# A linear-attention and ReGLU kernel on one core: half-row first loads, a first group made on TensorE, sketches in 16 tiles, one store per group, and a fixed issue order

## The chip, the cores and the metric

The kernel runs on one core of a Trainium2 chip. The metric is device time in microseconds (us) of that core, start to end of one execution of the program. Shapes are fixed. Engines are named as in the profile: PE is TensorE, DVE VectorE, ACT ScalarE, POOL GpSimd, and SP the sequencer that issues most DMAs.

## What is computed

```python
batch, n_heads, seq, head_dim = (4, 4, 1088, 32);  r = 8
def phi(x):
    a = np.einsum('rd,bhsd->bhsr', S1, x)
    b = np.einsum('rd,bhsd->bhsr', S2, x)
    return np.einsum('bhsi,bhsj->bhsij', a, b).reshape(*x.shape[:-1], r * r)
q_p, k_p = (phi(q), phi(k))
kv = np.einsum('bhsf,bhsd->bhfd', k_p, v)
z = np.sum(k_p, axis=2)
num = np.einsum('bhsf,bhfd->bhsd', q_p, kv)
den = np.einsum('bhsf,bhf->bhs', q_p, z)[..., None] + 1e-06
attn = num / den
x = attn.transpose(0, 2, 1, 3).reshape(4352, 128)
out = (np.maximum(x @ w_gate, 0.0) * (x @ w_val)) @ w_out     # d_ff = 1536
```

Two sketches of eight columns each make 64 features per head (phi). Sums over all tokens of a batch give kv and z, so no row of attn of a batch can be made before all of its k and v has gone through. The result, 4352 tokens of 128, goes through a gated feed-forward network (FFN) of width 1536. Inputs and output are float32; features and FFN are fp16 inside.

## The kernel before

**Tokens.** The 1088 tokens of a batch are 34 chunks of 32 rows, each row of SBUF holding one head's row of 34 x 32 numbers. Thirty-two chunks form 8 columns of four (x = 0 to 7), two are left over. The FFN takes tokens in ten groups, written (batch, first x, number of x): (0,0,2), (0,2,2), (0,4,4), then (b,0,4) and (b,4,4) for b = 1 to 3, and a group of 256 that collects the left-over chunks of all batches. The first group is small, so that the FFN may begin early.

**k side, class K, once a batch.** DVE transposes k in 32 x 32 blocks (L389, L393, L397). PE makes both sketches with the block-diagonal weights wS (L405, L416: 64-row by 32-column tiles, eight of which cover the array), DVE transposes back (kt2, L425). PE sums z (L434), DVE copies it (L442), PE and DVE make of z a third sketch matrix wc (L445, L450), by which q gives the denominator. The feature products kphi (L456) are made on DVE and POOL, ACT casts v to fp16 (L462, L466), PE makes kv (L473), DVE masks and scales it (L480).

**q side, class Q, once a group.** PE makes the two sketches (L586) and the third (L595) from the transposed q; DVE transposes back (L603, L611); the product of second and third sketch (L617, bw), its sum (L624), the reciprocal (L629) and the division of the first sketch by it (L633) follow, then the feature product (L640). Early groups do these on DVE, the others on POOL. The features are transposed by PE and ACT (L656, L661) for batch 0, by a DMA (L648) for the rest; PE multiplies by kv (L669, L676), and ACT writes xT (L684).

**FFN, class F.** 102 units of 512 result columns: PE makes the gate (g, L730) and the value (v, L741), ACT takes relu of g (L735), DVE multiplies it with v (h, L750). In 13 units ACT copies v (L746) and POOL multiplies (L754). Four matmuls of w_out (L761) add up in one PSUM bank per group; ACT scales that into SBUF (oe, L769), and SP stores it: four DMAs of 32 rows a group (L776), eight for the left-over group (L784).

**What sets the order.** Each step is an operation of a planner (class Plan) with a cost, a due time and PSUM banks to lease from seven; a list scheduler fixes at build time the order in which each engine's instructions are issued. Matmuls of zeros (L263) go to the eighth bank: 34 at the start, six after the S matmuls, and as many as fit into planned gaps of PE ahead of the first FFN matmul, 100 in all.

**Loads.** ACT and SP each issue one load of S1 and S2 (L203, L204). SP then loads k of batch 0 whole (L205) and q of batch 0 in three parts (L220, L221, L223); ACT's queue loads v (L189, L195). POOL's loads the weights: w_gate and w_val in three blocks of four column tiles each (L236, L237), w_out in one. A `gate` copy on POOL (L799) holds back the loads of the later batches (L805, L808), which SP issues.

Of the kernel before, what the change touches and what calls it, by code (L numbers as in the profile page):

```python
# [17 lines left out]
EPS = 1e-6  # L18


class Lease:


    def __init__(self, n=1):
        self.n, self.banks, self.free_at, self.left = n, None, None, 0


class Op:
    def __init__(self, eng, name, busy, vis, fn, after, take, drop, due):
        self.eng, self.name, self.busy, self.vis, self.fn = eng, name, busy, vis, fn  # L30
        self.after = [a for a in after if a is not None]
        self.take, self.drop, self.due = take, drop, due
        self.succ, self.start, self.done, self.seq = [], None, None, None


class Plan:


    HOLD = 1.0
    LAT = {"PE": 0.20, "DVE": 0.035, "ACT": 0.035, "POOL": 0.06, "SP": 0.0, "DMA": 0.05}  # L40

    def __init__(self, free, banks):
        self.free = dict(free)
        self.banks = {b: 0.0 for b in banks}
        self.ops = []

    def add(self, eng, name, busy, fn, after=(), take=(), drop=(), rec=0.0, due=None):
        op = Op(eng, name, busy, busy + rec + self.LAT[eng], fn, after, take, drop, due)
        op.seq = len(self.ops)
        for l in drop:  # L50
            l.left += 1
        for a in op.after:
            a.succ.append(op)
        self.ops.append(op)
        return op

    def look(self, o):
        return 0.0

    def landed(self, name, at):  # L60
        op = self.add("DMA", name, 0.0, None)
        op.start, op.done = at, at
        return op

    def dues(self, slack):
        for op in reversed(self.ops):
            lim = [s.due - op.vis - slack(op, s) for s in op.succ if s.due is not None]
            if op.due is not None:
                lim.append(op.due)
            op.due = min(lim) if lim else 1e6  # L70

    def run(self):
        todo = [o for o in self.ops if o.start is None]
        need = {o: sum(a.start is None for a in o.after) for o in todo}
        ready = [o for o in todo if not need[o]]
        n = 0
        while ready:
            for o in ready:
                o.at = max([self.free[o.eng]] + [
                    a.start + a.busy if a.eng == o.eng == "PE" else a.done for a in o.after])  # L80
            have = sorted(self.banks.values())
            now = min(o.at for o in ready)

            held = 0
            wants = sorted((o for o in ready if any(l.banks is None for l in o.take)),
                           key=lambda o: (o.due, o.seq))
            for o in wants:
                w = sum(l.n for l in o.take if l.banks is None)
                near = o.at <= now + self.HOLD
                if held + w > len(have):  # L90
                    o.at = None
                else:
                    o.at = max(o.at, have[held + w - 1])
                if near:
                    held += w
            can = [o for o in ready if o.at is not None]
            if not can:
                raise RuntimeError("no bank for any of " + ", ".join(o.name for o in ready))
            o = min(can, key=lambda o: (o.at, o.due, o.seq))

            o = min((c for c in can if c.eng == o.eng and c.at <= o.at + self.look(o)),
                    key=lambda c: (c.due, c.seq))
            o.start = o.at
            o.done = o.start + o.vis
            self.free[o.eng] = o.start + o.busy
            for l in o.take:
                if l.banks is None:
                    got = sorted(self.banks, key=lambda b: (self.banks[b], b))[:l.n]
                    l.banks = sorted(got)
                    for b in got:  # L110
                        del self.banks[b]
            for l in o.drop:
                l.left -= 1
                l.free_at = max(l.free_at or 0.0, o.done)
                if not l.left:
                    for b in l.banks:
                        self.banks[b] = l.free_at
            ready.remove(o)
            for s in o.succ:
                need[s] -= 1  # L120
                if not need[s]:
                    ready.append(s)
            n += 1
        assert n == len(todo), [o.name for o in todo if o.start is None]
        return max(o.done for o in todo)
# [3 lines left out]
def kernel(  # L129
# [25 lines left out]
    LAG = 3  # L155
# [3 lines left out]
    f_g = ctx.enter_context(tc.tile_pool(name="f_g", bufs=6))  # L159
    f_h = ctx.enter_context(tc.tile_pool(name="f_h", bufs=10))  # L160
# [6 lines left out]


    s16 = sb([2 * R, 4, D], FP32, "s16")
    k_sb = [sb([128, NC * D], FP32, f"k_sb{b}") for b in range(B)]  # L170
    q_sb = [sb([128, NC * D], FP32, f"q_sb{b}") for b in range(B)]
    v32 = [sb([128, H, NX * D], FP32, f"v32_{b}") for b in range(B)]
# [3 lines left out]
    wv = sb([DM, NJ, 128], FP16, "wv")  # L176
    wo = sb([128, NJ, DM], FP16, "wo")
# [4 lines left out]
    xT = sb([HD, B * NX * 128 + 256], FP16, "xT")  # L182


    def flat(src, b):
        return src[b].rearrange("h (p c) d -> (h p) (c d)", c=NC)

# [12 lines left out]
    def wcols(w, lo, hi):  # L200
        return w.rearrange("m (j f) -> m j f", j=NJ)[:, lo:hi]

    nc.scalar.dma_start(out=s16[0:R], in_=S1[:, None, :].to_broadcast([R, 4, D]))  # L203
    nc.sync.dma_start(out=s16[R:2 * R], in_=S2[:, None, :].to_broadcast([R, 4, D]))  # L204
    nc.sync.dma_start(out=k_sb[0], in_=flat(k, 0))  # L205
    zero = sb([128, 128], FP16, "zero")
    nc.vector.memset(zero, 0.0)
    scr = sb([1, 1], FP16, "scr")
    nc.scalar.activation(out=scr, in_=zero[0:1, 0:1], func=ACTF.Relu)
    for a in range(4):  # L210
        load_v(nc.scalar, 0, a)
    for a in range(2):
        load_vr(nc.scalar, a, 0, 1)

    Q0 = 2 * D

    def by_x(t, lo, hi):
        return t[:, 0:4 * NX * 32].rearrange("p (a c) -> p a c", a=4)[:, :, lo * 32:hi * 32]

    nc.sync.dma_start(out=by_x(q_sb[0], 0, 2), in_=by_x(flat(q, 0), 0, 2))  # L220
    nc.sync.dma_start(out=by_x(q_sb[0], 2, NX), in_=by_x(flat(q, 0), 2, NX))  # L221
    qrest = slice(4 * NX * 32, NC * 32)
    nc.sync.dma_start(out=q_sb[0][:, qrest], in_=flat(q, 0)[:, qrest])  # L223

    id16 = sb([2 * R, 2 * R], FP32, "id16")
    make_identity(nc, id16)
    sel = sb([2 * R, 16, R], FP32, "sel")
    nc.gpsimd.tensor_copy(out=sel, in_=id16[:, None, 0:R].to_broadcast([2 * R, 16, R]))
    maskl = sb([128, 4, 4], FP32, "maskl")
    nc.gpsimd.memset(maskl, 1.0)  # L230
    nc.gpsimd.affine_select(out=maskl, in_=maskl, compare_op=ALU.is_ge, fill=0.0, base=0,
                            pattern=[[-8, 4], [-32, 4]], channel_multiplier=1)
    nc.gpsimd.affine_select(out=maskl, in_=maskl, compare_op=ALU.is_ge, fill=0.0, base=R - 1,
                            pattern=[[8, 4], [32, 4]], channel_multiplier=-1)
    for lo in range(0, NJ, 4):
        nc.gpsimd.dma_start(out=wg[:, lo:lo + 4], in_=wcols(moe_w_gate, lo, lo + 4))  # L236
        nc.gpsimd.dma_start(out=wv[:, lo:lo + 4], in_=wcols(moe_w_val, lo, lo + 4))  # L237
    nc.gpsimd.dma_start(out=wo, in_=moe_w_out.rearrange("(j f) m -> f j m", f=128))
    ident = sb([128, 128], FP16, "ident")
    make_identity(nc, ident)  # L240


    maskp = sb([128, 2], FP32, "maskp")
    maskw = sb([128, H, R], FP32, "maskw")
    maskkv = sb([128, 2, D], FP32, "maskkv")
    nc.vector.memset(maskp, 0.0)
    nc.vector.memset(maskw, 0.0)  # L247
    nc.vector.memset(maskkv, 0.0)
    for h in range(H):
        nc.vector.memset(maskp[32 * h:32 * h + 32, h % 2:h % 2 + 1], 1.0)  # L250
        nc.vector.memset(maskw[32 * h:32 * h + 32, h], DSCALE)
    for i in range(2):
        nc.vector.memset(maskkv[64 * i:64 * i + 64, i], KVSCALE)
    NBW = 3
    bw = [sb([128, GX * H, R + 1], FP32, f"bw{i}") for i in range(NBW)]
    for i in range(NBW):
        nc.vector.memset(bw[i][:, :, R], EPS * DSCALE)

    W_BANK = 7
# [31 lines left out]
    def pe16(n, cols):  # L291
        return n * max(cols / 2400.0 + 0.0025, 0.0285)
# [626 lines left out]
```

## Time and profile before

| what | value |
|---|---|
| time, median of 3 runs | 121.84 us (121.58 to 121.86) |
| span of the profiled execution | 119.8 us |
| time of a run outside that span (median less span) | 2.0 us |
| busy: PE, PEld, DVE, ACT, POOL | 105.0, 69.6, 85.9, 79.4, 60.8 us |
| first FFN matmul (L730) | 21.11 us |
| last instruction of ACT ahead of the last stores | 113.51 us |

The profile is one execution, taken by the hardware profiler. Busy time is summed per engine; PEld are the weight loads, which overlap the matmuls. The chain of waits is followed back from the last instruction to what released it, step by step, and gives each engine and line a share of the span. The timeline gives start, duration, engine, line, operation, result and operands of each instruction or run of equal ones; `[0.39 <-PE ...]` behind it says how long the engine stood idle before it and who released it. The stretches give busy time of each engine, number of instructions in brackets, the granted PE clock and the DMA share. The DMA view counts packets by size and, for each queue, packets, MB and the share of the time of all 16 DMA engines in the stretch.

### The profile page before, as it was taken

How to read it: one execution, taken by the hardware profiler on the slowest of the kernel's cores; microseconds unless marked ns; L12 is line 12 of the kernel's file. 1: busy time of each engine (PE TensorE's matmuls, PEld its weight loads, DVE VectorE, ACT ScalarE, POOL GpSimd, SP SyncE). 2: the span in 40 equal slices, each digit the busy share in tenths (PEclk: the TensorE clock that was granted, in tenths of full speed). 3: DMA queues.
4: the chain of work that ended last, by engine and by line, in shares of the span. 5: the costliest groups of instructions: out<-in, count | busy, mean ns of one | idle time of the engine just before them, and what ended most of it. 6: DMA issues, size and time to landing. Idle time of an engine off the chain costs nothing.

```text
span 119.8 us, 3483 instructions
## 1 busy us (share of the span) xinstructions
PE 105.0 (88%) x1354; PEld 69.6 (58%) x1354; DVE 85.9 (72%) x196; ACT 79.4 (66%) x152; POOL 60.8 (51%) x75
## 2 busy tenths in 40 slices
PE   6966996998997959989999899998999999999600
PEld 6954866795755626445566564665656656569300
DVE  2169558599997969988999586876858858776600
ACT  4003102899785855869958669896799799998500
POOL 7938206800967189636542997595095262332100
PEclk9999999999999999999999999999999999999985
DMA  2999999999931508230421071105204302300310
GB/s 48 273 229 218 204 312 252 275 242 307 242 90 32 108 0 50 43 88 0 87 68 25 10 86 45 45 5 112 63 0 96 88 3 44 70 23 0 88 27 16
DMA packets 17104, 12.02 MB, mean 100 GB/s; under 512 B 11456, under 2 KB 15296, under 8 KB 17088
## 3 DMA queue, kind: packets, MB, share of 16 engines
q1 hardware_dynamic: 13768, 10.07, 37.6%
q0 software_dynamic: 2416, 1.18, 7.3%
q10 hardware_dynamic: 904, 0.56, 2.2%
q8 instruction: 10, 0.16, 0.7%
q14 instruction: 6, 0.05, 0.2%
HBM read 9.05 MB, written 2.23 MB: 94 GB/s over the span
## 4 chain that ended last, share of the span: by engine, by line
PE 69%; DMA 8%; ACT 7%; DVE 7%; issue 2%; DVEq 1%; ACTq 0%
PE ps L730 19%; PE ps L741 17%; PE ps L761 17%; DMA v<-in_v_dram 7%; ACT g_sb L735 3%; PE ps L595 3%; PE ps L586 3%; PE ps L473 3%; PE ps L669 2%; DVE kab L425 2%; ACT v L462 2%; DVE qab L603 2%; PE ps L434 1%; DMA s<-in_S_dram 1%; DVE ht L750 1%
## 5 line engine op out<-in xcount | busy, mean ns | idle before, releaser
L735 ACT ACTIVATE g_sb<-ps 128x512 f16<-128x512 f32 x102 | 58.4, 610 | 15.3 <-PE ps L730 13.0
L750 DVE TENSOR_TENSOR ht<-g_sb,ps 128x512 f16<-128x512 f16 x89 | 57.4, 678 | 13.1 <-PE ps L730 5.5
L730 PE MATMUL ps<-xT,wg 128*128 128x512 f16 (+1 forms) x120 | 38.8, 348 | 2.7 <-DVE kab L425 1.5
L741 PE MATMUL ps<-xT,wv 128*128 128x512 f16 (+1 forms) x120 | 38.8, 348 | 0.7 <-DVE kab L425 0.4
L761 PEld LDWEIGHTS <-ht 128*128 128x128 f16 x408 | 28.6, 98 | 17.2 <-issue 3.1
L761 PE MATMUL ps<-wo,ht 128*128 128x128 f16 x408 | 36.8, 219 | 0.8 <-DVE ht L750 0.4
L754 POOL TENSOR_TENSOR ht<-g_sb,v_sb 128x512 f16<-128x512 f16 x13 | 15.0, 1156 | 15.1 <-ACT v_sb L746 15.0
L456 POOL TENSOR_TENSOR kp<-kab 128x512 f16<-128x512 f32 (+1 forms) x14 | 16.4, 1200 | 8.7 <-DVE kab L425 8.7
L640 POOL TENSOR_TENSOR qqp<-qan,qab 128x1024 f16<-128x1024 f32 (+2 forms) x10 | 16.4, 1643 | 5.5 <-DVE qan L633 5.0
L741 PEld LDWEIGHTS <-wv 128*128 128x128 f16 x120 | 11.3, 98 | 6.9 <-issue 3.8
L730 PEld LDWEIGHTS <-wg 128*128 128x128 f16 x120 | 11.6, 99 | 4.7 <-issue 2.3
L263 PE MATMUL ps<-zero 128*128 128x128 f16 x100 | 9.7, 272 | 1.1 <-DVE maskw L247 1.1
L633 POOL TENSOR_TENSOR qan<-qab,qrd 128x128 f32<-128x128 f32 (+1 forms) x8 | 3.1, 394 | 13.8 <-DVE qrd L629 10.9
L462 ACT CAST v<-v 128x512 f16<-128x512 f32 x8 | 4.7, 628 | 7.9 <-DMA v<-in_v_dram 7.9
L263 PEld LDWEIGHTS <-zero 128*128 128x128 f16 x100 | 8.2, 125 | 1.8 <-DVE maskw L247 1.1
L746 ACT CAST v_sb<-ps 128x512 f16<-128x512 f32 x13 | 7.7, 590 | 0.0
L603 DVE STREAM_TRANSPOSE qab<-ps 128x256 f32<-128x256 f32 (+1 forms) x10 | 4.0, 405 | 4.7 <-PE ps L595 2.7
L473 PEld LDWEIGHTS <-kp 128*128 128x128 f16 (+1 forms) x72 | 4.8, 107 | 3.4 <-issue 1.7
L473 PE MATMUL ps<-v,kp 128*128 128x64 f16 (+1 forms) x72 | 5.6, 204 | 1.3 <-ACT v L462 1.0
L661 ACT COPY qpt<-ps 128x512 f16<-128x512 f16 (+1 forms) x3 | 2.2, 727 | 6.9 <-PE ps L656 6.8
L617 POOL TENSOR_TENSOR bw<-qab,qc 128x128 f32<-128x128 f32 (+1 forms) x8 | 3.5, 440 | 6.0 <-DVE qc L611 5.0
L769 ACT ACTIVATE o_sb<-ps 128x512 f32<-128x512 f32 (+1 forms) x10 | 5.5, 550 | 1.4 <-PE ps L761 1.4
(70 smaller groups left out, 86.1 us busy)
## 6 DMA issues: line engine op xcount, KB each, us to landing
k_sb<-in_k_dram SPq DMA_DIRECT2D x4, 544.0 KB, 6.6
out_dram<-o_sb SPq DMA_DIRECT2D x28, 64.0 KB, 1.7
q_sb<-in_q_dram SPq DMA_DIRECT2D x3, 544.0 KB, 7.8
v<-in_v_dram SPq DMA_DIRECT2D x12, 128.0 KB, 7.2
v<-in_v_dram ACTq DMA_DIRECT2D x4, 128.0 KB, 5.4
wg<-in_moe_w_gate_dram POOLq DMA_DIRECT2D x3, 128.0 KB, 8.4
q_sb<-in_q_dram SPq DMA_DIRECT2D x1, 384.0 KB, 9.1
wv<-in_moe_w_val_dram POOLq DMA_DIRECT2D x3, 128.0 KB, 8.6
```

The source lines that it names most:

```text
L263: nc.tensor.matmul(PS[:, W_BANK, 0:128], zero, zero, start=True, stop=True)
L456: eng.tensor_tensor(out=self.kp[:, lo:hi].rearrange("p x g (i a c) -> p (x g i) a c", i=2, a=R), in0=src[:, 0, :, :, None].to_broadcast([1 ...
L462: nc.scalar.copy(out=v16[self.b][:, 2 * h:2 * h + 2, 0:NX * D], in_=v32[self.b][:, 2 * h:2 * h + 2])
L473: nc.tensor.matmul(m[:, 64 * p:64 * p + 64], self.kp[rows, x, p], v16[self.b][rows, 2 * p:2 * p + 2, x * D:(x + 1) * D], start=(x == 0 and ...
L640: eng.tensor_tensor(out=self.qp[:, lo:hi].rearrange("p x g (i a c) -> p (x g i) a c", i=2, a=R), in0=self.an[:, lo * H:hi * H, :, None].to ...
L730: nc.tensor.matmul(bank(self.lg)[:, y * W:(y + 1) * W], wg[:, j], x, start=True, stop=True, skip_group_check=True)
L735: nc.scalar.activation(out=self.gs, in_=bank(self.lg), func=ACTF.Relu)
L741: nc.tensor.matmul(bank(self.lv)[:, y * W:(y + 1) * W], wv[:, j], x, start=True, stop=True, skip_group_check=True)
L746: nc.scalar.copy(out=self.vs, in_=bank(self.lv))
L750: nc.vector.tensor_tensor(out=self.ht, in0=self.gs, in1=bank(self.lv), op=ALU.mult)
L754: nc.gpsimd.tensor_tensor(out=self.ht, in0=self.gs, in1=self.vs, op=ALU.mult)
L761: nc.tensor.matmul(o[:, s], self.ht[:, y * W + s * 128:y * W + (s + 1) * 128], wo[:, j], start=(j == 0 and s == 0), stop=(j == NJ - 1), sk ...
```

## The change

- **Order.** The list scheduler goes. A table START gives the rank of every operation, BANKS the PSUM banks of each lease (all eight now), WARM the places of 39 matmuls of zeros in place of 100. Dependencies are as the code states them; each engine takes its operations by rank.
- **First loads.** k and q of batch 0 are loaded in two parts of half rows (`half`, L256), the first half holding 16 chunks; v of batch 0 in eight smaller loads. In SP's order the first half of k is followed by that of q. Both loads of S go to ACT's queue.
- **First group.** Class First makes the features of group (0,0) directly in the layout that kv needs: `feat` (L645) multiplies q with sketch matrices that are widened to all 64 pairs (wab), once for the first and once for the second factor; ACT copies one, DVE multiplies (L616). The transposes of features by PE go there. The denominator is made on its own path (the first sketch with z, L673), turned into a [feature, token] tile by a widened copy, a PE transpose and a copy, and multiplied in where x is written (L637), behind kv.
- **k side of batch 0.** For two of the kphi products ACT copies the second sketch to PSUM (L533), and DVE reads it there (L539).
- **q sketches.** Once a batch, not once a group, all three sketches side by side as one matrix wq of 32 columns; 16 matmuls of 32 rows by 32 columns by 256 tokens (L761). Transposes, sums and reciprocals of a batch's both groups are made together.
- **Weights.** wg and wv are laid out [128, 3, 128, 4] and read by PE with a step of 4 elements (L884), so that each of their loads is one run per row; w_out comes in three loads.
- **Stores.** One DMA for a group of 128 x 512 (L927), two on SP and two on ACT for the left-over group (L933).
- **Buffers.** g_sb 8 in place of 6, ht 12 in place of 10; k_sb and v32 two in place of four, shared by b and b + 2. Thirteen units go to POOL as before, others of them.

The core of the diff:

```diff
-    def run(self):
-        todo = [o for o in self.ops if o.start is None]
...
+    def run(self, warm):
+        order = sorted(self.ops, key=lambda o: (START[o.seq] if START else 0, o.seq))
+        for o in order:
+            if o.seq in WARM:
+                warm(WARM[o.seq])
+            o.fn()
...
-    wg = sb([DM, NJ, 128], FP16, "wg")
+    wg = sb([DM, 3, 128, 4], FP16, "wg")
...
-    nc.sync.dma_start(out=k_sb[0], in_=flat(k, 0))
+    def half(t, src, y):
+        lo, hi = (0, CY) if y == 0 else (CY, NC * D)
+        return lambda: nc.sync.dma_start(out=t[:, lo:hi], in_=flat(src, 0)[:, lo:hi])
...
+        def feat(self, l, w):
+            for p in range(2):
+                rows = slice(64 * p, 64 * p + 64)
+                for x in range(self.n):
+                    nc.tensor.matmul(
+                        bank(l, p)[:, x * 128:(x + 1) * 128], wab[rows, w].rearrange("p g i j -> p (g i j)"),
+                        by_x(qT[0], x, x + 1)[rows], start=True, stop=True,
+                        skip_group_check=True)
...
+            rb = P.add("ACT", "f rb", lambda: nc.scalar.copy(
+                out=self.rb, in_=self.rd[:, :, None].to_broadcast([128, n * H, D])), [o3])
+            rt = P.add("PE", "f rt", lambda: self.rt(lx), [rb, fidf], take=[lx])
...
+            self.x_op = P.add("DVE", "f x", lambda: nc.vector.tensor_tensor(
+                out=xT[:, 0:n * 128], in0=bank(ln)[:, 0:n * 128], in1=self.rT, op=ALU.mult),
...
+        def sk(self, ls):
+            for h in range(H):
+                rows = slice(32 * h, 32 * h + 32)
+                o = bank(ls[h // 2], h % 2)
...
+                            nc.tensor.matmul(
+                                o[32 * a:32 * a + 32, (lo - self.x0) * 32:(hi - self.x0) * 32],
+                                wq[self.b][rows, h],
...
-                nc.tensor.matmul(bank(self.lg)[:, y * W:(y + 1) * W], wg[:, j], x,
+                nc.tensor.matmul(bank(l)[:, y * self.W:(y + 1) * self.W], w[:, j // 4, :, j % 4],
...
-                for a in range(4):
-                    nc.sync.dma_start(
-                        out=out[b * S:(b + 1) * S].rearrange("(p c) m -> p (c m)", c=NC)[
-                            :, (a * NX + x0) * DM:(a * NX + x0 + n) * DM],
-                        in_=self.os[32 * a:32 * a + 32, 0:n * DM])
+                dst = rows.rearrange("p (a x) m -> a p x m", a=4)[:, :, x0:x0 + n]
+            nc.sync.dma_start(out=dst.rearrange("a p x m -> a p (x m)"),
+                              in_=self.os[:, 0:n * DM])
...
+                eng.dma_start(
+                    out=out[b * S:(b + 1) * S].rearrange("(p c) m -> p c m", c=NC)[
+                        :, 4 * NX:NC].rearrange("p e m -> e p m"),
+                    in_=self.os[p0:p0 + 64, y * DM:(y + 1) * DM])
```

More of the change, by code (lines that the diff above doesn't have):

```diff
@@ L31, in __init__ @@
         self.after = [a for a in after if a is not None]
-        self.take, self.drop, self.due = take, drop, due
-        self.succ, self.start, self.done, self.seq = [], None, None, None
+        self.take, self.drop = take, drop
 class Plan:
[L39 to L53, printed above, removed]
+    def __init__(self):
+        self.ops, self.leases = [], []
@@ L54, in add @@
+    def add(self, eng, name, fn, after=(), take=(), drop=()):
+        op = Op(eng, name, fn, after, take, drop, len(self.ops))
         self.ops.append(op)
         return op
[L57 to L70, printed above, removed]
@@ L72, in run @@
-    def run(self):
-        todo = [o for o in self.ops if o.start is None]
[L74 to L125, printed above, removed]
@@ L235 @@
[L235 to L246, printed above, removed]
@@ new lines, with fill4 @@
+    f3 = P.add("DVE", "sel", fill3, [fid, f0])
+    def fill4():
+        nc.vector.tensor_reduce(out=mz, in_=maskl, axis=AX.X, op=ALU.add)
+    f4 = P.add("DVE", "mz", fill4, [fml])
+    l_s, l_x = Lease(P), Lease(P)
+    st_op = P.add("PE", "st", lambda: nc.tensor.matmul(
+        bank(l_s)[:, 0:2 * R], s16.rearrange("f p d -> f (p d)"), id16, start=True, stop=True),
+        [ls1, ls2, fid, f0], take=[l_s])
+    ws_op = P.add("DVE", "ws", lambda: nc.vector.tensor_tensor(
+        out=wS, in0=bank(l_s)[:, 0:2 * R].rearrange("p (w i) -> p w i", w=2)[
+            :, :, None, :].to_broadcast([128, 2, 2, R]),
+        in1=maskp[:, None, :, None].to_broadcast([128, 2, 2, R]), op=ALU.mult), [st_op, f1])
@@ new lines, with mk_wq @@
+    s1r_op = P.add("POOL", "s1r", mk_s1r, [stc, f1])
+    sx_op = P.add("PE", "sx", lambda: nc.tensor.matmul(
+        bank(l_x)[:, 0:D], sel.rearrange("f a i -> f (a i)"), s16[:, 0], start=True, stop=True),
+        [ls1, ls2, f3], take=[l_x])
+    l_op = P.add("ACT", "L", lambda: nc.scalar.copy(
+        out=L, in_=bank(l_x)[:, None, 0:D].to_broadcast([128, H, D])), [sx_op], drop=[l_x])
+    def mk_wq(b):
+        nc.gpsimd.memset(wq[b][:, :, 24:32], 0.0)
+        nc.gpsimd.tensor_copy(
+            out=wq[b][:, :, 0:16],
+            in_=s_t.rearrange("p w i -> p (w i)")[:, None, :].to_broadcast([128, H, 2 * R]))
@@ new lines, in __init__ @@
+            for (lo, hi, rest), t1 in zip(parts, t1s):
+                la = Lease(P, 2)
+                s = P.add("PE", f"ksk {b} {lo}",
+                          lambda la=la, lo=lo, hi=hi, rest=rest: self.sk(la, lo, hi, rest),
+                          t1 + [ws_op, f2], take=[la])
+                self.sks.append(s)
+                self.t2s.append(P.add(
+                    "DVE", f"kt2 {b} {lo}",
+                    lambda la=la, lo=lo, hi=hi + rest: self.t2(la, lo, hi), [s] + pu, drop=[la]))
@@ new lines, in vcr, with kv @@
+        def vcr(self):
+            nc.scalar.copy(out=v16[self.b][0:64, :, NX * D:KX * D], in_=vr32[:, self.b])
+        def kv(self, lm, lo, hi):
+            m = bank(lm)
+            for x in range(lo, hi):
+                for p in range(2):
+                    nc.tensor.matmul(
+                        m[:, 64 * p:64 * p + 64], self.kp[:, x, p],
+                        v16[self.b][:, 2 * p:2 * p + 2, x * D:(x + 1) * D],
+                        start=(x == 0 and p == 0), stop=(x == NX), skip_group_check=True)
@@ new lines, in t2, with at @@
+        def t2(self, la):
+            nc.vector.transpose(
+                self.ab.rearrange("p w x h f -> p h x w f"),
+                pair(la)[:, :, 0:self.n * 32].rearrange("p h (x w f) -> p h x w f", w=2, f=16))
+        def at(self, l):
+            for x in range(self.n):
+                nc.tensor.matmul(
+                    bank(l)[:, x * 128:(x + 1) * 128], s1r.rearrange("p r h i -> p (r h i)"),
+                    by_x(qT[0], x, x + 1), start=True, stop=True, skip_group_check=True)
@@ new lines, in csk, with mul @@
+        def csk(self, lc):
+            for x in range(self.n):
+                nc.tensor.matmul(
+                    bank(lc)[:, x * 32:(x + 1) * 32], self.aT[:, x * 128:(x + 1) * 128],
+                    self.kk.zs.rearrange("p h r -> p (h r)"), start=True, stop=True,
+                    skip_group_check=True)
+        def mul(self, lc):
+            nc.vector.tensor_tensor(
+                out=self.bw[:, :, 0:R],
+                in0=self.ab[:, 1].rearrange("p x g (i r) -> p (x g i) r", r=R),
+                in1=bank(lc)[:, 0:self.n * 32].rearrange("p (x r) -> p x r", r=R), op=ALU.mult)
@@ L666, in num, with tre @@
+        def tre(self, lt, lo, m):
+            o = bank(lt).bitcast(FP16)
+            nc.scalar.copy(out=self.pt[:, lo:lo + m].rearrange("f x g t -> f (x g t)"),
+                           in_=o[:, 0:m * 256])
+        def num(self, ln, lo, m):
+            o = bank(ln)
             for p in range(2):
@@ L857, with warm @@
-    P.ops.sort(key=lambda o: o.seq)
-    order, seen = [], set()
-    def visit(o):
-        if o in seen:
-            return
-        seen.add(o)
-        for a in o.after:
-            visit(a)
-        order.append(o)
-    import sys
-    sys.setrecursionlimit(100000)
-    for o in P.ops:
-        visit(o)
-    P.ops = order
-    P.dues(slack)
-    end = P.run()
+    def warm(n):
+        for _ in range(n):
+            nc.tensor.matmul(PS[:, 7, 0:128], zero, zero, start=True, stop=True,
+                             skip_group_check=True)
@@ L876 @@
     if __name__ != "kernel":
         kernel.plan = P
-        kernel.end = end
-    todo = sorted((o for o in P.ops if o.fn), key=lambda o: (o.start, o.seq))
-    f0 = min(o.start for o in P.ops if o.name.startswith("g "))
-    at = None
-    for o in todo:
-        if o.eng == "PE":
-            if at is not None and o.start < f0 + 0.1 and o.start - at > 0.3:
-                warm(int((o.start - at - 0.1) / 0.065))
-            at = o.start + o.busy
-        o.fn()
+        if not START:
+            return
@@ L892 @@
+    P.run(warm)
 _INS = ['q', 'k', 'v', 'S1', 'S2', 'moe_w_gate', 'moe_w_val', 'moe_w_out']
```

983 lines of the change are left out of this document (500 added, 483 removed), and 70 rows, old and new, of tables (BANKS, START).

## The prediction

> **What bounds the kernel now.** I read the chain of waits first, then the timeline up to the first FFN matmul, the busy time by stretches, and the DMA view of the first loads and of the end.
>
> ```profile
> PE 105.0 (88%) x1354; PEld 69.6 (58%) x1354; DVE 85.9 (72%) x196; ACT 79.4 (66%) x152; POOL 60.8 (51%) x75
> PE 69%; DMA 8%; ACT 7%; DVE 7%; issue 2%; DVEq 1%; ACTq 0%
> ```
>
> PE carries 69% of the chain, so the end is set by PE's stream; the shares are averages over three stages, which I cost apart.
>
> ```profile
> 6.24 1.29 DVE L389 STREAM_TRANSPOSE kT<-k_sb 128x512 f32<-128x512 f32 x2
> ...
> 16.66 0.32 DVE L603 STREAM_TRANSPOSE qab<-ps 128x128 f32<-128x128 f32 x1 [1.16 <-PE ps L595]
> ...
> 20.69 0.37 ACT L684 CAST xT<-ps 128x256 f16<-128x256 f32 x1 [0.39 <-PE ps L669]
> ...
> 21.11 0.38 PE L730 MATMUL ps<-xT,wg 128*128 128x256 f16 x2
> ```
>
> Stage A, start to 21.1 us: loads, then a DVE chain of small steps. All of it is on the path: L730 waits for xT.
>
> ```profile
> 21.10:70.00 48.90, 45.53 (x609) 28.70 (x607) 41.75 (x84) 37.60 (x73) 28.57 (x29) 1.00 0.49 104
> 70.00:107.00 37.00, 36.61 (x416) 22.14 (x415) 27.81 (x53) 32.81 (x63) 19.66 (x20) 1.00 0.24 52
> ```
>
> Stage B, 21.1 to 113.5 us (columns after the stretch's length: PE, PEld, DVE, ACT, POOL): PE is nearly always occupied, DVE 85% in the first stretch, ACT 89% in the second. ACT's 89% is about the best that this pipeline sustains.
>
> ```profile
> 113.51 0.38 ACT L769 ACTIVATE o_sb<-ps 128x256 f32<-128x256 f32 x1 [1.42 <-PE ps L761]
> 113.92 3.57 SPq L784 DMA_DIRECT2D out_dram<-o_sb  x8
> ```
>
> Stage C, 113.5 to 119.8 us: eight stores issued one by one, 6.3 us after PE's last result.
>
> **Stage A after.** The searched order puts the first halves of k and q ahead on SP. By the page's GB/s row (slices of 3 us: 48, 273, 229) 0.14 MB have moved by 3 us and 0.96 by 6. The first q half follows all of k, 0.82 MB: 5.5 us if SP's queue gets everything, 8.2 if it shares evenly from 4.1 us on. I take 6.9. In DVE's new order kt2, kphi and everything behind them queue behind this q transpose. The sum of DVE from there, with the durations of the same shapes: transposes 0.40 + 0.45 + 0.42 + 0.30 + 0.47; two kphi of 512 elements and the new feature product at 0.68 each (the h product L750, which also reads one operand from PSUM, takes 0.68, while L456 with both in SBUF took 1.18); zc 0.15; the rest of q 0.73; bw, sum, reciprocal 0.59; four transposes 1.48; sum and reciprocal of the next groups 0.39, ahead of "f x" in the queue; f x 0.40 as L684. That is 7.8 us. DVE's waits for PE now between 7.5 and 17 us are about 3.9 (0.95, 0.74, 0.88, 1.16, small ones). The chain through sketch, wc and qsk stays, the transposes through PSUM and the qphi of the first group go; I keep half, 2.0. First g: 6.9 + 7.8 + 2.0 + 0.2 = **16.9**, 4.2 earlier. Ends: 15.0 (no waits left) and 19.0 (all kept). Hidden: the transformed matrices on ACT and POOL behind the q load; kv and kve behind DVE's chain.
>
> A new wait: SP's loads of the second v halves and, behind them, the second q half (SP row 9) wait for earlier DMAs to land. DVE reaches its transpose at about 12; q's long part landed at 11.25 before. A later landing moves the start by as much, inside the 19.0.
>
> What is late next is the clock. The dummies tell it: 34 weight loads in 3.54 us at the start are 104 ns each, against 11 in 0.66 us (60 ns) at 19.46. Spacing halves at about 16.9 us, four us ahead of the first g now. After, there are 39 dummies in place of 100 and PE waits more, so the first 3 us of FFN may run at half rate: at most 3 us / 2 = 1.5 us, partly under waits for x; I take 1.0 (ends 0 and 2).
>
> **Stage B after.** The units: 102 x (g + v + four o), each step 0.22 from start to start (54.28, 54.50, 54.72 in the timeline), 66.8 us. Unchanged in number.
>
> ```profile
> 49.96 0.45 PE L586 MATMUL ps<-qT,wS 64*32 64x128 f32 x16
> 50.34 0.43 PE L595 MATMUL ps<-qT,wc 128*32 128x128 f32 x8
> 50.69 0.39 PE L741 MATMUL ps<-xT,wv 128*128 128x512 f16 x1
> ...
> 65.16 0.66 PE L405 MATMUL ps<-kT,wS 64*32 64x256 f32 x16
> 65.62 0.27 PE L416 MATMUL ps<-kT,wS 64*32 64x32 f32 x16
> ```
>
> Per batch: q sketches 2 x 0.73, k sketch 0.66, z 0.57, w 0.30, kv 0.55, num 0.68: 4.2; three batches 12.7; transposes, nums and the left-over tokens 2.1. Together 81.6 of the 92.4 us, so 10.8 us of stall, most before 70 us.
>
> The 16-tile sketch: eight tiles at 128 columns take 0.38, four take 0.36, eight at 256 columns 0.46. Time goes with the columns of one tile, hardly with the tiles. Sixteen matmuls of 256 columns, one a tile: 0.46 if sixteen run side by side, 0.92 if as twice eight; I take 0.60. Three batches: 3 x (1.46 - 0.60) = 2.6 less; the left-over tokens 0.2 more. PE's need: 79.2.
>
> Stall: ACT needs 75.5 us and DVE 74 in this stage (sums of the stretches), and nothing there changes by over 1 us (13 units on POOL as before). At 89% ACT alone gives 84.8. With one more PSUM bank, more buffers and the mixed order I take 6.3 of stall and 1.0 for the clock: 79.2 + 7.3 = **86.5** (84 to 90).
>
> **Stage C after.** Stores now have 4 outer rows (rest: 2) on the DRAM side. How many DMA engines serve a DMA shows in its completion packets of 4 bytes:
>
> ```profile
> DMA packets 80, 0.01 MB, mean 32 GB/s; under 512 B 80, under 2 KB 80, under 8 KB 80
> ...
> DMA packets 384, 0.13 MB, mean 22 GB/s; under 512 B 128, under 2 KB 384, under 8 KB 384
> ...
> q1 hardware_dynamic: 192, 0.26, 37.8%
> ```
>
> First line, 1.7 to 1.96 us: two loads of s, 8 outer rows x 4 pieces, 64 packets and 16 completions, 8 each. Second, 113.9 to the end: eight stores of 32 rows, 256 packets and 128 completions, 16 each. So 8 outer rows get 8 engines, and I expect 4 for a store and 2 for a store of the rest. [...] Third line, 111 to 114 us: 37.8% of 16 x 3 us for 128 packets of 2 KB, 0.142 us each. The k load (4352 bytes in 0.167 at 14.7 to 16 us, the share 78.8% over 98 packets) gives 0.079 for 2 KB. I take 0.10. One store is then 32 packets on each of four engines, 3.2 us; a store of the rest 32 packets of 512 B, at 0.03, 0.96 us, four of them on the same engines.
>
> Order at the end, T being PE's last result: the store of group (3,0) starts moving at T - 1.2, the one of (3,4) queues behind it, the four small ones behind that: 2 x 3.2 + 4 x 0.96 = 10.2, T + 9.0. The last packet now lies at 118.2, 1.6 before the end. T + **10.6** (ends 8.0 and 14.0). So the single store costs 4.3 us here, though it saves SP's issue time. In the middle SP's order keeps the transposing DMAs ahead of the stores, and three output buffers cover them.
>
> **Sum.** 16.9 + 86.5 + 10.6 = 114.0, against a span of 119.8: -5.8. Around the span lie 2.0 us (121.84 - 119.8, the median; the runs spread 121.58 to 121.86), so **116.0 us**.
>
> **Rivals.**
> 1. The stores use all sixteen engines. For: a 128-row source. Against: the s loads. Then the last small store's data is out at about T + 2.6: T + 4.2, 107.6, measured 109.6. Chance 0.2.
> 2. Slower: wg and wv are read with a step of 4 elements. A weight load takes 98 ns in L730's and L741's rows, under 216 ns of a 512-column and 109 ns of a 256-column matmul, and no row here has a stepped load. At twice 98 the 72 narrow matmuls each show 0.087 us, 6.3 us: 122.3. It decides from 190 ns a load; at four times it costs 49 us. [...] Chance 0.1.
> 3. Slower: store packets stay at 0.142 us. Three stores ahead of the store that frees the output buffer of group (3,0) then end 3 us after it is wanted, and the tail is 14.0: 103.4 + 3 + 14.0 + 2.0 = 122.4. Chance 0.08.
> 4. The change doesn't start FFN earlier (second q half late, clock half): start 19, stage B 88.5: 120.1. Chance 0.1.
>
> The forecast itself, 113 to 119.5: 0.52. Range 109 to 122: it reaches to rival 1 and to the bounds of stages A to C. A difference of 0.3% is about what can be told from none. Faster 0.81 (forecast, rival 1, most of 4), slower 0.17 (2, 3, a tenth of slack), same 0.02.
>
> **What would show it.** First L884 matmul at 15 to 19 us; the L761 sketches at 0.5 to 0.9 us a batch; weight loads at 98 ns; completions of 4 and 2 in the store's packets, and 9 to 14 us from PE's last matmul to the end. If that tail is under 5 us, stage C is wrong; if PE ends after 107 us, stage B.

## The result and the profile after

The changed kernel takes **130.69 us** (median of six runs, 130.25 to 131.79) against 121.76: ratio 1.0744, 95% interval 1.0691 to 1.0797. The forecast was 116.0, within 109 to 122. Three single runs below, one each of e1, e2 and g2, took over 1.5% longer than the fastest of their kernel, and the medians leave them out. From the page of the changed kernel, busy times and the chain's shares by engine:

```profile
PE 102.5 (79%) x1293; PEld 71.9 (55%) x1293; DVE 87.0 (67%) x190; ACT 80.5 (62%) x163; POOL 62.4 (48%) x87
...
PE 51%; DVE 16%; ACT 12%; DMA 5%; issue 4%; SPq 1%; DVEq 1%; ACTq 0%
```

PE is busy for less time than before (102.5 for 105.0 us; its matmuls of zeros alone fell from 9.7 to 4.7) in a longer span (130.0 for 119.8), so it stands idle for 27.5 us where it was 14.8. DVE's share of the chain went from 7% to 16%. So the time went into waits, not into more work. The stretches from the first FFN matmul to 70 us, from there to PE's end, and from there to the end (columns: PE, PEld, DVE, ACT, POOL, granted clock, DMA share, GB/s):

```profile
22.50:70.00 47.50, 41.09 (x547) 27.20 (x545) 40.64 (x77) 35.40 (x71) 31.39 (x34) 1.00 0.40 94
70.00:118.10 48.10, 44.44 (x512) 30.42 (x509) 35.33 (x62) 38.53 (x74) 18.16 (x19) 0.96 0.20 46
118.10:130.00 11.90, 0.02 (x1) 0.00 (x0) 0.00 (x0) 0.38 (x1) 0.00 (x0) 0.67 0.17 54
```

PE, which worked 93% and 99% of the two stretches shown for the kernel before (21.1 to 70 and 70 to 107 us), works 87% and 92% of the first two here. By term, all from traces:

| term | before | forecast | after | e2 | e3 | f2 | f4 |
|---|---|---|---|---|---|---|---|
| first FFN matmul (stage A) | 21.1 | 16.9 | 22.3 | 21.2 | 22.2 | 20.2 | 19.8 |
| from there to PE's end (B) | 92.4 | 86.5 | 95.8 | 87.0 | 85.7 | 85.1 | 88.3 |
| PE's end to the end (C) | 6.3 | 10.6 | 11.9 | 12.0 | 12.2 | 6.3 | 6.3 |
| median time less span of the profiled run | 2.0 | 2.0 | 0.7 | 1.7 | 0.4 | 2.4 | 2.5 |
| time | 121.8 | 116.0 | 130.7 | 121.9 | 120.5 | 114.1 | 117.0 |

(e2 to f4 are experiments below.) The miss of 14.7 us is 9.3 in stage B, 5.4 in stage A, 1.3 in stage C, and 1.3 the other way in the row above the time. That row is no stage: each of the changed kernel's six runs took 1.7 to 1.8 us more than its own span, but the profiled one is the slowest of them (131.79 us). So the three stages are here together 1.1 us longer than in the median run.

**Where stage B waits.** What PE waited for, 23 to 118 us; first the kernel before, then the changed one (us in total, times, longest):

```profile
PE ps L730 <- DVE kab L425: 1.5, 2, 1.1
PE ps L730 <- DVE qab L603: 0.8, 2, 0.6
PE ps L741 <- DVE kab L425: 0.4, 1, 0.4
```

```profile
PE ps L884 <- DVE qabc L777: 3.6, 4, 1.3
PE ps L884 <- DVE kab L503: 1.1, 1, 1.1
PE ps L820 <- DVE kab L503: 1.1, 1, 1.1
PE ps L832 <- DVE qabc L777: 1.0, 1, 1.0
PE ps L908 <- DVE kab L503: 0.7, 1, 0.7
PE ps L908 <- DVE qabc L777: 0.7, 1, 0.7
```

Lines 777 and 503 transpose the sketches of q and k. The FFN's matmuls (L884, L908) read nothing that they write; nor do the transposes of q's features (L820) and their product with kv (L832), which here wait for a transpose of another batch. That makes 8.2 us of waits for a stranger, 2.7 in the three lines of before. One of them in the timeline of the changed kernel:

```profile
75.66 0.38 PE L884 MATMUL ps<-xT,wg 128*128 128x512 f16 x1
...
76.14 0.60 ACT L889 ACTIVATE g_sb<-ps 128x512 f16<-128x512 f32 x1
76.77 0.72 DVE L777 STREAM_TRANSPOSE qabc<-ps 128x512 f32<-128x512 f32 x1 [1.74 <-ACT g_sb L889]
...
77.54 1.14 PE L884 MATMUL ps<-xT,wg 128*128 128x512 f16 x3 [1.27 <-DVE qabc L777]
```

By the table BANKS the transpose at 76.77 reads banks 0 and 4 with one step over both. Its operands were ready at 74.05, when PE's sketch ended. The matmul at 75.66 fills bank 2, relu empties it, and the transpose waits for that relu; the matmul at 77.54 fills bank 1, and waits for the transpose. Banks 1 and 2 lie between 0 and 4, and it touches neither. This looks as if such a read is taken as one range, bank 0 through bank 4, when the program's waits are made; e2 and e3 below test it. That it waits even for a relu, a read against a read, is what this timeline shows (1.74 us, released by ACT's L889); why, no run shows.

The stall is followed by a slower clock. The same stretch in two windows (granted clock third from the end):

```profile
74.00:76.00 2.00, 0.97 (x15) 0.56 (x8) 0.85 (x2) 1.08 (x3) 1.15 (x1) 1.00 0.18 15
...
78.00:80.00 2.00, 2.00 (x9) 1.03 (x8) 1.46 (x5) 0.98 (x2) 1.63 (x4) 0.50 0.13 50
```

In the first window PE worked half the time. From 77.9 to 81.3 the granted clock was 0.50, and each 512-column matmul stepped by 0.43 us, not 0.22; an estimate from these figures is 1.7 us more of stage B. The trace of e3 has no such fall behind its first FFN units until PE has ended (granted clock 1.00 from 22 to 107 us).

### The profile page after: what moved, and what is told of

The parts are those of the page before. It is cut to its first block, busy times and chain, and to the rows that moved or that the text cites. A ratio compares the mean times of both kernels' runs of the same rounds, so it can differ in the third digit from the quotient of the medians.

```text
span 130.0 us, 3276 instructions
## 1 busy us (share of the span) xinstructions
PE 102.5 (79%) x1293; PEld 71.9 (55%) x1293; DVE 87.0 (67%) x190; ACT 80.5 (62%) x163; POOL 62.4 (48%) x87
## 4 chain that ended last, share of the span: by engine, by line
PE 51%; DVE 16%; ACT 12%; DMA 5%; issue 4%; SPq 1%; DVEq 1%; ACTq 0%
PE ps L884 25%; PE ps L908 12%; ACT g_sb L889 8%; DVE ht L897 7%; DMA q_sb<-in_q_dram 5%; DVE qabc L777 4%; PE ps L761 3%; PE ps L645 2%; DVE kab L503 2%; PE ps L832 2%; PE ps L567 1%; DVE kT L483 1%; ACT qpt L824 1%; ACT o_sb L916 1%; PE ps L981 1%
## 5 line engine op out<-in xcount | busy, mean ns | idle before, releaser
L889 ACT ACTIVATE g_sb<-ps 128x512 f16<-128x512 f32 x102 | 56.2, 606 | 13.1 <-PE ps L884 10.6
L884 PE MATMUL ps<-xT,wg 128*128 128x512 f16 (+1 forms) x120 | 36.7, 358 | 4.2 <-DVE qabc L777 3.6
L908 PEld LDWEIGHTS <-ht 128*128 128x128 f16 x408 | 29.7, 99 | 17.5 <-issue 7.1
L908 PE MATMUL ps<-wo,ht 128*128 128x128 f16 x408 | 36.7, 221 | 1.6 <-DVE kab L503 0.7
L884 PE MATMUL ps<-xT,wv 128*128 128x512 f16 (+1 forms) x120 | 36.2, 356 | 1.4 <-DVE kab L503 1.1
L539 POOL TENSOR_TENSOR kp<-kab 128x512 f16<-128x512 f32 (+2 forms) x15 | 16.8, 1128 | 4.0 <-DVE kab L503 4.0
L884 PEld LDWEIGHTS <-wg 128*128 128x128 f16 x120 | 13.0, 116 | 7.0 <-issue 4.6
L805 POOL TENSOR_TENSOR qqp<-qan,qabc 128x1024 f16<-128x1024 f32 (+1 forms) x9 | 15.8, 1755 | 0.6
L884 PEld LDWEIGHTS <-wv 128*128 128x128 f16 x120 | 12.9, 116 | 4.7 <-issue 1.8
L785 POOL TENSOR_TENSOR bw<-qabc 128x128 f32<-128x128 f32 (+1 forms) x9 | 3.7, 423 | 12.4 <-DVE qabc L777 12.4
L799 POOL TENSOR_TENSOR qan<-qabc,qrd 128x128 f32<-128x128 f32 (+1 forms) x9 | 3.4, 380 | 12.2 <-DVE qrd L795 12.2
L777 DVE STREAM_TRANSPOSE qabc<-ps 128x512 f32<-128x512 f32 (+2 forms) x12 | 6.0, 524 | 4.5 <-ACT g_sb L889 1.7
L845 ACT CAST xT<-ps 128x512 f16<-128x512 f32 (+1 forms) x9 | 4.9, 540 | 5.6 <-DVE qabc L777 2.6
L567 PEld LDWEIGHTS <-kp 128*128 128x128 f16 x72 | 4.7, 110 | 2.6 <-issue 1.2
L567 PE MATMUL ps<-v,kp 128*128 128x64 f16 x72 | 5.4, 205 | 0.9 <-DVE qabc L777 0.9
L981 PE MATMUL ps<-zero 128*128 128x128 f16 x39 | 4.7, 312 | 1.1 <-DVE maskh L309 1.1
L954 DVE STREAM_TRANSPOSE qT<-q_sb 128x544 f32<-128x544 f32 (+1 forms) x7 | 5.2, 736 | 0.0
L981 PEld LDWEIGHTS <-zero 128*128 128x128 f16 x39 | 3.9, 146 | 1.3 <-DVE maskh L309 1.1
```

Source lines behind the costliest of these rows:

```text
L539: eng.tensor_tensor(out=self.kp[:, lo:hi].rearrange("p x g (i a c) -> p (x g i) a c", i=2, a=R), in0=a[:, :, :, None].to_broadcast([128, n ...
L567: nc.tensor.matmul(m[:, 64 * p:64 * p + 64], self.kp[:, x, p], v16[self.b][:, 2 * p:2 * p + 2, x * D:(x + 1) * D], start=(x == 0 and p == ...
L777: nc.vector.transpose(self.abc[:, lo:lo + m, 2 * i2:2 * i2 + 2].rearrange("p x h f -> p h x f"), pair(ls[i2])[:, :, lo * 32:(lo + m) * 32] ...
L805: nc.gpsimd.tensor_tensor(out=self.qp[:, lo:hi].rearrange("p x g (i a c) -> p (x g i) a c", i=2, a=R), in0=self.an[:, lo * H:hi * H, :, No ...
L884: nc.tensor.matmul(bank(l)[:, y * self.W:(y + 1) * self.W], w[:, j // 4, :, j % 4], x, start=True, stop=True, skip_group_check=True)
L889: nc.scalar.activation(out=self.gs, in_=bank(l), func=ACTF.Relu)
```

## The experiments

Edits are against the changed kernel, where nothing else is said. Two theories for stage B: **1**, a read over two banks is ordered against all banks between; **2**, the fixed order was made for other durations, and its waits stay whatever the banks.

**e1, stores as before.**

```diff
-            nc.sync.dma_start(out=dst.rearrange("a p x m -> a p (x m)"),
-                              in_=self.os[:, 0:n * DM])
+            for a in range(4):
+                nc.sync.dma_start(out=dst[a].rearrange("p x m -> p (x m)"),
+                                  in_=self.os[32 * a:32 * a + 32, 0:n * DM])
```

(The left-over group likewise, in eight.)

> The changed kernel, its stores cut as before: four DMAs of 32 rows a group, eight for the left-over tokens (four on SP, four on ACT). If the tail of 11.9 us after PE's last result comes from the few DMA engines that serve a store (4 and 2, by its completions), each store gets 16 engines again, the last packet lies about 5 us after the last copy to SBUF, and the time falls by 5 to 6 us, to about 125. Rival: the tail is the queue behind the writes to DRAM, whatever cut they have, and SP's eight issues of 0.45 us come on top: within 1 us of 130.7 or slower.

Measured: 124.69 us, 1.028 [1.021, 1.035] of before: 6.0 less than the changed kernel. The DMA view from 118 us on (changed kernel), and from 116 us on (this one):

```profile
DMA packets 520, 0.65 MB, mean 54 GB/s; under 512 B 16, under 2 KB 272, under 8 KB 519
```

```profile
DMA packets 757, 0.63 MB, mean 91 GB/s; under 512 B 256, under 2 KB 512, under 8 KB 757
```

Bytes are the same. Small packets are completions: 16 for six stores (4 + 4 + 4 x 2) against 256 for sixteen (16 each). They agree with the busy share: at 106 to 113 us, where such stores of the changed kernel move, their packets fill 24.2% of 16 engines, 3.9 of them. With few engines the tail is 11.9 us, with sixteen 6.3. The forecast's reading of stage C holds.

**e2, banks renamed.**

```diff
-        self.banks = BANKS[self.id] if BANKS else list(range(n))
+        self.banks = sorted(SWAP[b] for b in BANKS[self.id])
+SWAP = (0, 3, 6, 5, 2, 7, 1, 4)
```

(The zeros' bank likewise.)

> The changed kernel with the eight PSUM banks renamed throughout (0,1,2,3,4,5,6,7 become 0,3,6,5,2,7,1,4); order, durations and every real dependency are unchanged, but the pairs of banks that one DVE transpose reads lie closer: 16 banks lie between the two of a pair in all, in place of 47. Theory 1: a read with a step over two banks is ordered against every operation on the banks between them, and these waits make up most of the 9 us that stage B takes more than forecast: 125 to 127.5. Theory 2: the waits come from a fixed order made for other durations, and the banks between do nothing: 130.2 to 131.2.

Measured: 121.87 us, 1.0015 [0.9983, 1.0046] of before: 8.8 us gone, by names alone, and more than theory 1 had. Order, work and real dependencies are those of the changed kernel, so theory 2 falls.

**e3, bank by bank.**

```diff
-            nc.vector.transpose(
-                self.abc[:, lo:lo + m, 2 * i2:2 * i2 + 2].rearrange("p x h f -> p h x f"),
-                pair(ls[i2])[:, :, lo * 32:(lo + m) * 32].rearrange("p h (x f) -> p h x f", f=32))
+            for i in range(2):
+                nc.vector.transpose(
+                    self.abc[:, lo:lo + m, 2 * i2 + i],
+                    bank(ls[i2], i)[:, lo * 32:(lo + m) * 32].rearrange("p (x f) -> p x f", f=32))
```

(And k's alike.)

> The changed kernel, the transposes of k's and q's sketches split into one instruction per bank, so that none spans banks; DVE does the same columns in twice as many instructions (0.73 us for 512 columns becomes two of about 0.42, some 0.1 us a pair more, about 1.3 us of DVE in all). Theory 1 (waits for the banks between): 124 to 127, below the kernel with renamed banks, since no bank lies between any more. Theory 2 (the order itself): 130.5 to 132, from the added DVE time.

Measured: 120.50 us, 0.992 [0.988, 0.996] of before: 10.2 less, again more than expected, although DVE got the longer work. Stage B is 85.7 us; the forecast had 86.5. All that the view lists of PE's waits in it, 23 to 118 us:

```profile
PE ps L512 <- DVE kab L504: 0.4, 1, 0.4
PE ps L834 <- ACT qpt L826: 0.3, 1, 0.3
PE ps L498 <- DVE kT L483: 0.2, 1, 0.2
PE ps L886 <- DVE zs L520: 0.2, 1, 0.2
```

The first three are real operands. In the last an FFN matmul still waits for a stranger (zs), for 0.2 us; the waits for the transposes are gone.

**e4, v's loads off ACT's queue.**

```diff
-lv0 = [[P.add("ACT" if a < 2 else "SP", f"ld v0{y}{a}",
-              lambda y=y, a=a: load_v0(nc.scalar if a < 2 else nc.sync, y, a))
+lv0 = [[P.add("ACT" if a < 2 and not y else "SP", f"ld v0{y}{a}",
+              lambda y=y, a=a: load_v0(nc.scalar if a < 2 and not y else nc.sync, y, a))
```

> The changed kernel, with the two loads of the second half of v that ACT issues moved to SP's queue. In the trace ACT stands from 3.3 to 8.5 us in front of such a load, which waits for the first q half to land, and the copies of the sketch matrices behind it, ready since 5.6 us, start at 8.5. If that is what makes the first group late, ACT's copies run 2.9 us earlier, PE's sketch of q and its features start at 8.6, no longer behind wab, and the first FFN matmul comes 0.5 to 1.0 us earlier: 129.7 to 130.2. Rival: the start hangs on the q half alone (landed at 8.1) and on DVE's chain behind it: within 0.3 us of 130.7.

Measured: 130.69 us. ACT's copies moved from 8.5 to 5.5 us as expected, and the first FFN matmul came at 22.55, no earlier: the theory fell, and the rival's time held.

**f1**, the edits of e1 and e3 together.

> The changed kernel with both edits that helped: the sketches' transposes bank by bank, and stores of 32 rows. The first edit acts on stage B and the second on the tail, so that they should add: 130.7 - 10.2 - 5.5 = 115.0, between 114.3 and 116. Were both gains the same slack counted twice (a store that frees a buffer late, and PE waiting for it), the sum would be less, 117 or above.

Measured: 115.39 us, 0.948 [0.943, 0.953]. The gains nearly add (15.3 of 16.2 us).

**f2, the first group's reads too**, against f1: the three reads of pairs in class First.

```diff
-                pair(la)[:, :, 0:self.n * 32].rearrange("p h (x w f) -> p h x w f", w=2, f=16))
+                    bank(la, i)[:, 0:self.n * 32].rearrange("p (x w f) -> p x w f", w=2, f=16))
...
-            fbe = P.add("ACT", "f fbe", lambda: nc.scalar.copy(out=self.fb, in_=pair(lfb)[:, :, 0:n * 128]), [fb],
+            fbe = P.add("ACT", "f fbe", lambda: [nc.scalar.copy(
+                out=self.fb[:, i], in_=bank(lfb, i)[:, 0:n * 128]) for i in range(2)], [fb],
```

(L616 likewise.)

> The kernel with both edits, and the three reads over two banks (0 and 6) in the first group split as well. There DVE's transpose of the sketch stands in front of banks 2 and 3, which PE fills with the widened features first: in the trace it starts 1.2 us after its own operand, and the next features 0.5 us behind it on PE. If the banks between make the first group late too, the first FFN matmul comes 0.5 to 1.5 us earlier and the time with it: 113.7 to 114.7. If PE's own chain at half rate sets the start, the 1.2 us are filled by other PE work and the time stays within 0.4 us of the kernel with both edits.

Measured: 114.05 us, 0.937 [0.931, 0.943]; first FFN matmul at 20.2. Such reads held the first group up, too; 1.3 us less than f1, inside its range. Two waits of PE that f1's trace still has, 0.5 us behind the sketch's transpose and 0.9 behind the product, are gone. (The two traces start FFN 1.8 us apart, but in f1's the half of q landed 0.4 us later.)

**f3, more zeros**, against f2.

```diff
-WARM = {35: 26, 70: 2, 272: 11}
+WARM = {35: 26, 70: 2, 160: 16, 162: 6, 169: 4, 272: 11}
```

> As the kernel with the first group split too, with 26 more matmuls of zeros in PE's gaps of the first stage: 16 ahead of the first group's sketch, 6 ahead of its a-sketch, 4 ahead of the transpose of the reciprocals. In the trace of the changed kernel PE runs at half rate until 20.8 us and again to 23.3 us, where the kernel before is at full rate from 16.9 us. If half rate makes the start late, the rate doubles some 4 us earlier, PE's work from 16 us on (sketches 1.9, transposes 1.0, zeros 1.3) takes half, and the first FFN matmul comes 1.5 to 2.5 us earlier: 112.5 to 113.5. If PE is not what the start waits for, the zeros do nothing or add their own 0.1 us each: 114 to 116.

Measured: 114.76 us. By the granted clock, full rate came at 8.9 us and went again at 15.8, after PE had waited for v's casts (0.79 us, up to 13.4), for the copy behind them (0.83, up to 14.5) and for q's second half (0.40; it landed at 15.0). It came back at 22.6, and the first FFN matmul stood at 20.8. So the clock was not tested where it counts.

**f4, the kernel before, bank by bank.**

```diff
-                PS[:, b0:b1 + 1:b1 - b0, lo * 32:hi * 32].rearrange("p h (x w f) -> p h x w f", w=2, f=16))
+                    bank(self.la, i)[:, lo * 32:hi * 32].rearrange("p (x w f) -> p x w f", w=2, f=16))
```

(In a loop over both banks; L603 likewise.)

> The kernel before, its transposes of two banks split bank by bank, nothing else. Its profile has 11 us of PE stall behind the first FFN matmul, and its transposes over two banks also stand in front of the banks between (17 between them in the trace's order, two to six banks apart). If these waits cost it too: 118.5 to 121. If they fall into other stalls there, DVE's added 0.1 us a pair is all: 121.5 to 122.5. What it gains is the part of the difference that the change did not bring but inherited.

Measured: 116.99 us, 0.961 [0.955, 0.967]: 4.7 us less than before, more than expected. No PE wait for these transposes is left in its trace.

**g1 to g4, the start**, against f2: ranks in START, and zeros.

```diff
+START[5] = 12.5                                     # g1, g2: q's second half (was 23)
+START[24], START[23], START[29] = 61.2, 61.4, 61.6  # g2: weight loads (were 27, 28, 29)
+START[168], START[92], START[93] = 84.1, 84.2, 84.3 # g3: first group ahead of rank 85
+START[169], START[170], START[171], START[172] = 84.4, 84.5, 84.6, 84.7
-WARM = {35: 26, 70: 2, 272: 11}
+WARM = {35: 26, 70: 2}                              # g3, g4
```

> The kernel with row stores and all reads split (114.05 us, first FFN matmul at 20.2), with the load of q's second half issued right behind the first in SP's order. There SP issued it at 9.7 us, behind loads of v that wait for earlier loads to land, and it landed at about 14.2; the second group's sketch, which needs it, stands ahead of the first group's last steps on PE. If the issue is what holds it, it lands by 12 and the first FFN matmul comes 1 to 2.5 us earlier: 111.5 to 113. Rival: the loads fill the DMA engines anyway, v's second half lands as much later, and PE's last kv steps wait for that: 113.6 to 115.

> As the kernel with q's second half early, with the last blocks of w_gate and w_val and the second of w_out (0.4 MB) issued by POOL behind the feature products, at about 12 us in place of 4 to 5.5. If the DMA engines are full between 2 and 14 us, the other loads land up to 1.8 us (0.4 MB at 225 GB/s) earlier: 0.5 to 1.8 us less than without this edit. If the loads wait for their issue and not for bandwidth, no difference within 0.4 us; and if the weights then land after PE wants them (19 us or later), 0.5 to 2 us more.

> The kernel with row stores and all reads split, with the first group's last steps (kv's last piece, reciprocal's transpose, kv times features, x) moved ahead of the second group's sketch on PE, ACT and DVE, and the 11 matmuls of zeros ahead of the first FFN matmul left out; the sketch (1.9 us at half rate) then stands between x's matmul and the FFN. If PE's order is what makes the start late, the first FFN matmul comes about 1.3 us earlier (the zeros), at 18.9: 112.7 to 113.4. If the first group's own steps wait for v's second half (landed at 13.2) and ACT's casts behind it, the order does little: 113.7 to 114.4.

> The kernel with row stores and all reads split, without the 11 matmuls of zeros ahead of the first FFN matmul. They take 1.3 us of PE at half rate after x's matmul; beside them lie DVE's write of x (0.42 us) and the wait for the transposed reciprocals. If they are only in the way: 0.5 to 0.8 us earlier, 113.2 to 113.6. If they bring the clock up for the first units, the gain is spent on half-rate matmuls: 113.9 to 114.6.

Measured: 115.79 (115.13 to 116.04), 114.67 (114.45 to 115.53), 115.16 (114.65 to 115.66) and 113.68 us (113.47 to 113.99), first FFN matmul at 21.7, 21.4, 21.0 and 19.6. g1: the start got later, past the rival's range too. One load displaced another here: with q's second half ahead, v's first half landed at 12.1 us, and SP's four issues of v took 7.6 us for 2.8 in f2. g2 overlaps g1: undecided. g3 is slower than either theory had it; its trace reaches full rate only at 25.2 us, f2's at 20.8. g4 starts 0.6 us earlier, and takes 1.1 longer in stage B: in its trace full rate comes at 24.2 us, so there the zeros bring it forward, as the second theory had it, though its time is f2's within their spreads. **f2 and g4 beat both kernels**: g4 is 0.935 [0.931, 0.939] of before.

## Why the prediction was wrong, point by point

**Stage B, the step that failed**: "With one more PSUM bank, more buffers and the mixed order I take 6.3 of stall and 1.0 for the clock". PE's need was right, the stall was not. Take PE's steps from start to start, and count as stall by how much each exceeds the median of its line and shape, where that is over 0.1 us. Behind the first FFN matmul this is 16.9 us in the changed kernel, which leaves 78.9 of 95.8 (forecast 79.2), where the forecast had 7.3 with the clock. With the reads split (e3) it is 7.9. So the missing 9 us are one mechanism: reads over two banks, seven of whose eight pairs in the q sketches of batches 1 to 3 and the left-over tokens lie at a distance of three or more (from BANKS). "One more PSUM bank" was counted as a gain; what the pairs' spread costs was not in the sum. No rival had this, though the page of before shows it: in the costliest groups, matmul L730 has its largest named idle time "<-DVE kab L425 1.5", a releaser that shares no data with it. I put it down to PE's stall and did not ask why. Of the 10.8 us of stall that the forecast read in the kernel before, 4.1 go in f4 (stage B 92.4 and 88.3). That e3 comes near 86.5 does not bear out the 6.3: the forecast took it without working, for a kernel with its reads unsplit.

The sketches run 0.71 us a batch (timeline at 50.36 us, L761), where I took 0.60: they gain as forecast, within 0.4 us for three batches.

**Stage A** failed, too: "In DVE's new order kt2, kphi and everything behind them queue behind this q transpose. The sum of DVE from there". The half of q landed at 8.1, not 6.9. But the sum was made over the wrong engine: the chain runs over loads, ACT and PE. In the changed kernel's trace PE waits three times for DVE on this way:

```profile
10.87 1.24 PE L645 MATMUL ps<-qT,wab 64*128 64x128 f32 x8 [0.50 <-DVE fab L661]
...
13.74 1.22 PE L667 MATMUL ps<-qT,s1r 128*128 128x128 f32 x4 [0.85 <-DVE fpt L616]
...
19.61 0.27 PE L567 MATMUL ps<-v,kp 128*128 128x64 f16 x2 [0.87 <-DVE qabc L777]
```

These 2.2 us go when the reads over two banks are split, the last with e3's edit, the others with f2's. In f2, with no such read left:

```profile
8.07 5.10 DMA v<-in_v_dram
...
14.09 0.28 ACT faT L624
...
15.69 1.88 PE ps L763 x50
...
19.15 1.29 PE ps L986 x11
```

v's second half lands at 13.2, ACT's casts of it stand ahead of a copy that PE waits for (L624), and PE takes 6.0 us (14.41 to 20.43) for the a-sketch, the second group's sketch, the reciprocals and the zeros, at half rate (the zeros take 117 ns each, and the first 256-column matmuls behind them step by 0.22 us, where 109 ns is the median). The forecast named the late second half and half rate, but bounded the first by 19.0 and charged the second to the FFN alone. The 3 us of FFN at half rate, from which its 1.0 us comes, were an estimate without a row behind it: in the changed kernel's trace full rate comes at 23.3, 1.0 behind the first FFN matmul. Of the 5.4 us, then, 2.1 go with these waits (22.3 to 20.2), and 3.3 are f2's 20.2 against 16.9. That ACT's copies stood behind its loads cost nothing that e4 could find. What the 3.3 would be at full rate stays open: f3 lost the rate again before it counted.

**Stage C** held: the cut was right (4 and 2 engines by the completions, 3.9 by the busy share), as e1 shows; the tail is 11.9 for 10.6, in its range of 8 to 14. It costs 5.6 us, not 4.3.

**The rivals.** Sixteen engines for a store: no, by the completions. Stepped weights:

```profile
L884 PEld LDWEIGHTS <-wg 128*128 128x128 f16 x120 | 13.0, 116 | 7.0 <-issue 4.6
```

116 ns for 99 before, but the steps of 512 and of 256 columns keep their old medians of 216 and 109 ns: they cost nothing visible. Slow store packets: no; at 106 to 113 us they take the 0.10 us that the forecast took (274 packets in 24.2% of 16 x 7 us). The late start came true, and later than its 19 us. The sign was wrong because the 8 to 10 us of stage B outweigh what the change saves; with them gone and the stores as before, the rest of the change is worth 2.9 us against the kernel before with its reads split (f2 against f4).

## What to carry to other kernels

Read who releases whom: where an instruction waits for one that writes nothing it needs, ask whether it is for a bank or buffer that both use, or was made by how an access is described. Try reading two PSUM banks in two instructions, or bring the pair's banks closer; here splitting the reads at two places gave 4.7 us to the old kernel and 10.2 to the new one, and 16 banks between the pairs in place of 47 gave the new one 8.8 (e2). The store that left as one DMA was cheap for SP to issue (0.53 us, against 1.7 for four) and, on 4 DMA engines by its completions, slow to finish, which counted at the end (a tail of 11.9 us, 6.3 with the stores as before).

## What the runs showed of the hardware

PE worked for 1.2 of the 3.5 us between 74.05 and 77.54; at 77.9 the granted clock fell to 0.50, and the matmuls of 512 columns stepped by 0.43 us in place of 0.22 for 3.4 us. In e3, without these waits, the granted clock is 1.00 from 22 to 107 us. That the stall brought the fall is read from these two traces; no run tested it alone.
